# A written-out order of work, searched anew, and new places for the loads of xT and of the first state (one core, attention and rational FFN)

## The chip, the cores and the metric

The kernel runs on one core of a Trainium2 chip. The metric is the time on the device of one execution, in microseconds (us), smaller is better. The engines are TensorE (PE in the profile, its weight loads PEld), VectorE (DVE), ScalarE (ACT), GpSimd (POOL) and the queue SP, which issues most DMAs.

## The reference

For each of 8 batches and 8 heads, 512 tokens `x` (64 wide) attend to 32 state rows, and the state rows attend to the tokens. All rows, 4608 in sum and 512 wide, go through a feed-forward layer whose activation is a quotient of two polynomials.

```python
scores = scale * x @ state.T                     # 512 x 32 per head
a = softmax(scores); xread = a @ state           # 512 rows of a batch
a2 = softmax(scale * state @ x.T); sread = a2 @ x  # 32 rows of a batch
h = rows @ w_in                                  # rows: 4608 x 512, w_in: 512 x 2048
P = a0 + a1*h + a2*h*h + a3*h*h*h
Q = 1 + |b0|*|h| + |b1|*h*h
out = (P / (Q + 1e-6)) @ w_out                   # w_out: 2048 x 512
```

## The kernel before, in words

The work of the feed-forward layer is cut into 72 units. Units 0 to 63 are batch b = n//8 and slice u = n%8 of 256 of the 2048 hidden columns, over that batch's 512 tokens; units 64 to 71 are the eight slices for the 256 state rows of all batches. `xread` is never formed: for four batch pairs and eight slices the state is first multiplied with `w_in` (token `X:i`, function `extra`, tile `ps_x`; `XA` copies the result out of PSUM to `xo` or `xo_w`, `xs` stores it, `lm` loads it again), and a unit's h is the softmax times that product (token `F:n:ci`, function `front`, tile `h`). Every number that TensorE multiplies here is split in a high and a low part, so `F` has 12 matmuls of 512 columns for a unit of tokens.

What happens in a unit n after `F`:

- ACT reads h twice: `FB` makes A = |b1|-scaled |h|, `FC` makes C, both 128x1024.
- DVE makes the polynomials: `qd`, `mu`, `po`. ACT takes the absolute value (`qa`).
- ACT makes the reciprocal 1/Q as exp(-ln Q): `ln` (function `recip_ln`, activation Ln) and `ex` (function `recip_exp`, activation Exp).
- DVE multiplies, `g1` gives the high part gh; `g2` and `g3` prepare the low part; POOL makes gl (`gl`).
- PE adds to four output accumulators o0 to o3 of the batch: `mh:n:t` is 4 matmuls of 512 columns with gh, `ml:n:t` 2 with gl.

The weights come as 64-bit floats and are made into 32 bits on the core: `lr` loads (512 KB a half), `cp` is a Prelu on ACT, `jr` and `jl` are two DVE instructions, `wh` (ACT) and `wl` (POOL) split a slice of `w_out`, `ws` stores a slice of `w_in`. The attention of a batch has its own tokens (`scores`, `sc_copy`, `row_...`, `col_...`, `e2_T`, `e2_copy`, `sread`, `sr_copy`, `sr_T`, `sr_fin`); batch 0 has its own variants that end in 0. `sread` needs `e2T`, which `e2_copy` writes on ACT.

PSUM has two tiles with the tag `h`, which `F`, `X`, the scores and `sread` take in turn: who takes one waits until everything that reads what was in it before is done.

Nothing is scheduled by the machine. The list ORDER holds 2337 tokens, and `tc.manual_schedule()` emits them one after the other; each engine runs its own instructions in that order, waiting where an input or a buffer is not ready. ORDER is therefore the order on every engine and queue at once. One token, `pre`, emits an explicit load of the ACT function table that holds both Ln and Exp; before the change it is the second token of the list (after the load of the first two batches' state), and in the instructions as built it is the only `ACT_TABLE_LOAD`. Where no such load stands ahead of an activation, the building step puts one in.

The loads of `xT` and `x` are 512 KB each (half a batch), and before the change both turn through the two buffers of one tag "x", in an order worked out from the list (token `lx`).

Of the kernel before, what the change touches and what calls it, by code (L numbers as in the profile page):

```python
# [18 lines left out]
P = 128  # L19
# [4 lines left out]
    "ls:0:2 pre lx scores0:0 sc_copy0:0 lr:0:0 cp:0:0 row_T0:0 jr:0:0 jl:0:0 row_max0:0 row_sub0:0 lx "  # L24
    "scores0:1 sc_copy0:1 row_T0:1 row_exp0:0 lr:0:1 cp:0:1 jr:0:1 ls:2:8 col_max:0 jl:0:1 "
    "col_scale:0 col_exp:0:0 col_exp:0:1 row_max0:1 row_sub0:1 row_exp0:1 row_sum0:0 row_norm0:0 X:1 "
    "row_sum0:1 lr:1:0 cp:1:0 lr:1:1 jr:1 X:0 XA:1 XA:0 fh:0 fo:0 cp:1:1 jl:1 X:2 a_T0:0 XA:2 lc cb "
    "cv a_hi0:0 a_lo0:0 row_norm0:1 a_T0:1 a_hi0:1 a_lo0:1 e2_T0:1 lr:2:0 cp:2:0 lr:2:1 b0a jr:2 "
    "cp:2:1 jl:2 X:4 fh:1 XA:4 lr:4:0 cp:4:0 lr:3:0 cp:3:0 lr:3:1 lr:4:1 cp:3:1 F:0:0 F:0:1 FB:0 fo:1 "
    "col_eps:0 col_norm:0 F:1:0 F:1:1 lr:5:0 jr:3 jl:3 xs:1 jr:4 FC:0 wh:3 wl:3:0 wl:3:1 FB:1 qd:0 "  # L30
    "qa:0 e2_T0:0 ln:0 ex:0 e2_copy0:0 e2_copy0:1 mu:0 qd:1 cp:5:0 po:0 lr:5:1 jr:5 cp:5:1 xs:0 lx lx "
    "sread:0:0 g1:0 mh:0:2 ws:0 cp:4:1 qa:1 FC:1 lr:7:0 xs:4 g2:0 sread:0:1 sr_copy:0 mh:0:3 jl:5 "
    "wh:5 sr_T:0 sr_fin:0 g3:0 ln:1 ex:1 ws:1 mu:1 po:1 lr:7:1 X:5 XA:5 X:8 XA:8 gl:0 ml:0:2 jl:4 "
    "g1:1 fh:2 lr:6:0 fo:2 cp:7:0 jr:7 cp:6:0 mh:0:1 cp:7:1 lr:6:1 cp:6:1 X:9 F:2:0 g2:1 xs:2 xs:5 "
    "XA:9 F:2:1 FB:2 FC:2 wl:5:1 wl:5:0 mh:1:1 jl:7 wh:7 ws:2 xs:8 g3:1 X:6 XA:6 jr:6 gl:1 mh:0:0 "
    "ml:0:0 qd:2 qa:2 ln:2 ml:0:3 mu:2 po:2 mh:1:0 jl:6 lr:9:0 wl:7:1 ex:2 g1:2 X:12 fh:3 XA:12 "
    "lr:9:1 cp:9:0 cp:9:1 X:10 lr:8:0 lr:8:1 ml:0:1 fo:3 jr:9 xs:6 wl:7:0 lr:11:0 lr:11:1 cp:8:0 jr:8 "
    "cp:8:1 xs:9 g2:2 XA:10 ml:1:2 jl:9 xs:10 mh:1:3 g3:2 gl:2 ml:1:3 F:3:0 F:3:1 FC:3 FB:3 ws:3 X:16 "
    "fh:4 ml:1:0 mh:2:1 lr:10:0 jl:8 mh:2:0 XA:16 lr:10:1 mh:1:2 ml:1:1 wh:9 wl:9:1 wl:9:0 lr:12:0 "
    "qd:3 qa:3 ln:3 xs:12 fo:4 lx mh:2:3 mu:3 ex:3 po:3 cp:11:0 jr:11 X:13 XA:13 X:14 XA:14 ml:2:2 "  # L40
    "cp:11:1 cp:10:0 cp:10:1 g1:3 ml:2:0 jr:10 F:4:0 xs:14 F:4:1 FB:4 lr:12:1 g2:3 FC:4 jl:11 xs:16 "
    "X:20 XA:20 mh:3:1 g3:3 gl:3 jl:10 fh:5 lr:13:0 lr:13:1 ml:2:1 wh:11 qd:4 mh:3:3 ml:2:3 xs:20 "
    "qa:4 ln:4 mh:2:2 fo:5 F:5:0 wl:11:0 ex:4 cp:12:0 cp:12:1 F:5:1 FC:5 mu:4 po:4 jr:12 ws:4 X:17 "
    "ml:3:1 g1:4 g2:4 wl:11:1 lr:14:0 mh:4:1 mh:3:2 lr:14:1 XA:17 xs:17 X:21 lx cp:13:0 jr:13 cp:13:1 "
    "FB:5 g3:4 XA:21 ml:3:3 xs:13 mh:3:0 jl:12 qd:5 gl:4 mu:5 cp:14:0 mh:4:3 cp:14:1 jr:14 mh:4:2 "
    "ml:4:1 xs:21 ml:3:2 po:5 qa:5 ln:5 ex:5 jl:13 ws:6 g1:5 jl:14 X:25 XA:25 ml:3:0 xs:25 lr:15:0 "
    "g2:5 scores:1:0 scores:1:1 sc_copy:1 tr1:1 wh:13 wl:13:1 X:24 wl:13:0 fh:6 fo:6 X:29 XA:29 xs:29 "
    "row_max:1 ml:4:2 wh:14 wl:14:0 lr:15:1 col_max:1 row_sub:1 XA:24 g3:5 mh:4:0 col_scale:1 F:6:0 "
    "F:6:1 lm:8 FB:6 lx mh:5:2 row_exp:1 cp:15:0 lx X:28 XA:28 lw:0 mh:5:1 xs:28 ml:4:3 mh:5:0 ml:4:0 "
    "row_sum:1 mh:5:3 gl:5 ml:5:1 ml:5:0 qd:6 row_eps:1 row_norm:1:0 cp:15:1 jr:15 ws:7 lm:10 "  # L50
    "row_norm:1:1 fh:7 fo:7 fs:8 F:7:0 ml:5:2 FC:6 mu:6 ml:5:3 po:6 col_exp:1:0 col_exp:1:1 qa:6 ln:6 "
    "jl:15 wl:14:1 ex:6 ws:5 tr2:1 X:3 XA:3 F:7:1 e2_T:1 a_hi:1 g1:6 g2:6 FB:7 mh:6:3 mh:6:2 FC:7 "
    "ft:8 lm:9 mh:6:0 g3:6 gl:6 e2_copy:1 sread:1:0 sread:1:1 mh:6:1 wh:15 col_eps:1 wl:15:1 qd:7 "
    "wl:15:0 col_norm:1 fs:10 sr_copy:1 sr_T:1 mu:7 ml:6:3 qa:7 sr_fin:1 a_lo:1 ml:6:1 ln:7 ex:7 "
    "F:8:0 F:8:1 FB:8 FC:8 po:7 g1:7 g2:7 g3:7 lw:3 ml:6:0 ml:6:2 mh:7:0 qd:8 fs:9 qa:8 lx lx ft:9 "
    "mh:7:1 mh:7:3 ln:8 ex:8 mu:8 po:8 g1:8 g2:8 mh:7:2 g3:8 F:9:0 F:9:1 FC:9 gl:7 FB:9 qd:9 ml:7:1 "
    "fl:7:1 ml:7:2 ml:7:3 fl:7:2 ml:7:0 fl:7:0 ft:10 F:10:0 F:10:1 fl:7:3 mh:8:1 mh:8:2 FB:10 mu:9 "
    "lm:11 po:9 gl:8 mh:8:0 ml:8:0 mh:8:3 lm:12 fs:12 FC:10 mu:10 ft:12 F:12:0 F:12:1 fs:11 ft:11 "
    "qa:9 ln:9 ex:9 FB:12 qd:10 qa:10 ml:8:3 po:10 F:11:0 F:11:1 FC:12 g1:9 mh:9:0 mh:9:2 xs:24 g2:9 "
    "g3:9 lw:6 mh:9:3 ml:8:1 qd:12 mh:9:1 gl:9 ml:9:2 lw:1 ml:9:1 ln:10 mu:12 ex:10 g1:10 g2:10 "  # L60
    "ml:8:2 FB:11 mh:10:3 mh:10:0 po:12 ml:9:3 FC:11 lm:13 fs:13 lm:15 ft:13 X:7 g3:10 gl:10 fs:15 "
    "qa:12 ft:15 mh:10:1 ml:9:0 ln:12 ex:12 xs:3 qd:11 mu:11 mh:10:2 XA:7 xs:7 ml:10:3 qa:11 ln:11 "
    "ml:10:2 lw:4 g1:12 mh:12:2 scores:2:0 ex:11 scores:2:1 po:11 g1:11 g2:11 g3:11 gl:11 sc_copy:2 "
    "col_max:2 X:15 XA:15 mh:12:0 lm:16 lw:2 F:13:0 F:13:1 FC:13 ml:10:0 tr1:2 row_max:2 row_sub:2 "
    "lm:14 lx lx fs:14 ft:14 mh:12:3 FB:13 qd:13 mh:11:3 X:11 XA:11 ml:11:1 xs:11 g2:12 row_exp:2 "
    "qa:13 ln:13 mh:11:2 col_scale:2 ex:13 ml:10:1 os:7:1 mh:12:1 ml:11:0 ml:11:3 F:14:0 col_exp:2:0 "
    "F:14:1 g3:12 col_exp:2:1 FB:14 gl:12 ml:12:0 ml:12:1 fs:16 ml:12:3 mu:13 po:13 g1:13 mh:13:0 "
    "F:15:0 F:15:1 g2:13 row_sum:2 row_eps:2 FC:14 mh:11:1 ml:11:2 os:7:0 qd:14 qa:14 row_norm:2:1 "
    "mh:13:3 ml:12:2 mh:13:2 ft:16 ln:14 ex:14 os:7:2 mh:11:0 row_norm:2:0 FB:15 mu:14 po:14 os:7:3 "
    "g3:13 mh:13:1 tr2:2 a_hi:2 e2_T:2 qd:15 qa:15 xs:15 lm:18 gl:13 ml:13:3 ml:13:0 e2_copy:2 FC:15 "  # L70
    "g1:14 mh:14:0 ln:15 a_lo:2 F:16:0 F:16:1 FC:16 mh:14:2 mh:14:3 g2:14 g3:14 mh:14:1 FB:16 gl:14 "
# [993 lines left out]
```

## Time and profile before

| | us |
|---|---|
| time, median of 3 runs (lowest, highest) | 664.37 (663.86, 664.41) |
| time of the execution that was profiled | 663.79 |
| its span, from the first to the last instruction | 662.0 |
| PE busy in the span | 644.4 |
| DVE busy | 624.6 |
| ACT busy | 521.4 |
| POOL busy | 314.3 |

The profiled execution's own time is 1.79 us longer than its span. An engine's busy time says how much of the span it was at work; what an engine waits for, and when, is read from the timelines and the windows. Line numbers are those of the kernel before; from the changed functions on the same lines of the changed kernel are numbered one or two away.

### The profile page before, as it was taken

How to read it: one execution, taken by the hardware profiler on the slowest of the kernel's cores; microseconds unless marked ns; L12 is line 12 of the kernel's file. 1: busy time of each engine (PE TensorE's matmuls, PEld its weight loads, DVE VectorE, ACT ScalarE, POOL GpSimd, SP SyncE). 2: the span in 40 equal slices, each digit the busy share in tenths (PEclk: the TensorE clock that was granted, in tenths of full speed). 3: DMA queues.
4: the chain of work that ended last, by engine and by line, in shares of the span. 5: the costliest groups of instructions: out<-in, count | busy, mean ns of one | idle time of the engine just before them, and what ended most of it. 6: DMA issues, size and time to landing. Idle time of an engine off the chain costs nothing.

```text
span 662.0 us, 11300 instructions
## 1 busy us (share of the span) xinstructions
PE 644.4 (97%) x4474; PEld 509.8 (77%) x4474; DVE 624.6 (94%) x585; ACT 521.4 (79%) x633; POOL 314.3 (47%) x174
## 2 busy tenths in 40 slices
PE   6699999999999999999999999999999999999997
PEld 2566767877877777877878888878878888888895
DVE  5999999999998999999999999999999999999886
ACT  5998989897869778878787778877787778687573
POOL 1164447545445165545444465436453555445541
PEclk9899999999999999999999999999999999999999
DMA  8979887316303365221123320431402201121401
GB/s 353 401 265 337 301 299 250 133 65 249 133 20 111 109 215 184 65 80 52 60 80 118 122 93 36 143 112 32 128 33 100 77 17 48 33 64 49 141 36 32
DMA packets 30679, 85.67 MB, mean 129 GB/s; under 512 B 3490, under 2 KB 3618, under 8 KB 30626
## 3 DMA queue, kind: packets, MB, share of 16 engines
q1 hardware_dynamic: 30290, 84.56, 36.6%
q8 instruction: 35, 0.57, 0.4%
q10 hardware_dynamic: 336, 0.39, 0.2%
q14 instruction: 18, 0.15, 0.1%
HBM read 57.15 MB, written 27.79 MB: 128 GB/s over the span
## 4 chain that ended last, share of the span: by engine, by line
PE 91%; ACT 3%; DVE 3%; issue 2%; DMA 1%; DVEq 0%
PE h L817 29%; PE ps_x L714 4%; PE o__2202 L890 2%; PE o__1510 L890 2%; PE o__1492 L890 2%; PE o__4162 L890 2%; PE o__4153 L890 2%; PE o__2245 L890 2%; PE o__2194 L890 2%; PE o__1517 L890 2%; PE o__3564 L890 2%; PE o__4771 L890 2%; PE o__2263 L890 2%; PE o__3531 L890 2%; PE o__5313 L890 2%; PE o__5820 L890 2%
## 5 line engine op out<-in xcount | busy, mean ns | idle before, releaser
L880 POOL TENSOR_TENSOR gl<-C,L 128x1024 fp32r<-128x1024 f32 (+1 forms) x70 | 176.0, 2514 | 252.7 <-DVE C L873 161.4
L817 PE MATMUL h<-aT,m 128*128 128x512 f32 x768 | 186.4, 391 | 0.8 <-DVE m L750 0.6
L817 PEld LDWEIGHTS h<-aT,m 128*128 128x128 f32 x768 | 143.3, 188 | 33.9 <-DVE m L750 1.7
L836 ACT ACTIVATE A<-h,cst 128x1024 f32<-128x1024 f32 (+1 forms) x72 | 76.9, 1070 | 43.4 <-PE h L817 37.4
L861 DVE SCALAR_TENSOR_TENSOR gh<-C,cst,L 128x1024 fp32r<-128x1024 f32 (+1 forms) x72 | 97.3, 1351 | 10.1 <-ACT L L937 8.1
L829 ACT ACTIVATE C<-h,cst 128x1024 f32<-128x1024 f32 (+1 forms) x72 | 83.4, 1159 | 25.8 <-PE h L817 19.0
L763 POOL TENSOR_TENSOR m<-m_sb,m 128x512 fp32r<-128x512 f32 x56 | 82.7, 1486 | 37.3 <-ACT m L759 33.7
L873 DVE SCALAR_TENSOR_TENSOR C<-C,cst,A 128x1024 f32<-128x1024 f32 (+1 forms) x72 | 89.2, 1242 | 1.5
L850 DVE SCALAR_TENSOR_TENSOR A<-A,b0a,h 128x1024 f32<-128x1024 f32 (+1 forms) x72 | 87.0, 1214 | 3.6 <-ACT A L836 2.6
L844 DVE SCALAR_TENSOR_TENSOR C<-C,cst,h 128x1024 f32<-128x1024 f32 (+1 forms) x72 | 87.7, 1218 | 1.7
L867 DVE SCALAR_TENSOR_TENSOR A<-A,gh 128x1024 f32<-128x1024 f32 (+1 forms) x72 | 85.8, 1193 | 1.5
L840 DVE TENSOR_TENSOR C<-C,h 128x1024 f32<-128x1024 f32 (+1 forms) x72 | 83.0, 1153 | 3.3 <-ACT C L829 2.0
L856 ACT ACTIVATE A<-A 128x1024 f32<-128x1024 f32 (+1 forms) x72 | 73.0, 1014 | 15.2 <-DVE A L850 14.5
L927 ACT ACTIVATE L<-A 128x1024 f32<-128x1024 f32 (+1 forms) x72 | 73.0, 1014 | 5.9 <-POOL gl L880 2.1
L937 ACT ACTIVATE L<-L 128x1024 f32<-128x1024 f32 (+1 forms) x72 | 72.9, 1014 | 1.8
L714 PE MATMUL ps_x<-win_sb,st 64*32 64x256 f32 x1024 | 36.3, 396 | 1.1 <-DVE C L844 0.4
L759 ACT CAST m<-m_sb 128x512 fp32r<-128x512 f32 x56 | 33.8, 615 | 0.0
L352 POOL TENSOR_TENSOR wo<-cv_r,wo 128x512 fp32r<-128x512 f32 x16 | 23.5, 1489 | 15.0 <-ACT wo L345 8.9
L714 PEld LDWEIGHTS ps_x<-win_sb,st 64*32 64x32 f32 x1024 | 17.6, 109 | 16.4 <-issue 5.8
L732 ACT COPY xo<-ps_x 128x1024 f32<-128x1024 f32 (+1 forms) x24 | 20.9, 875 | 5.1 <-PE ps_x L714 4.9
L817 PEld LDWEIGHTS h<-sh,m 128*128 128x128 f32 x192 | 24.1, 191 | 0.6
L817 PE MATMUL h<-sh,m 128*128 128x256 f32 x192 | 24.3, 283 | 0.0
(244 smaller groups left out, 1104.0 us busy)
## 6 DMA issues: line engine op xcount, KB each, us to landing
m_sb<-m_dram SPq DMA_DIRECT2D x56, 256.0 KB, 3.3
xT_sb<-in_xT_dram SPq DMA_DIRECT2D x16, 512.0 KB, 4.7
x_sb<-in_x_dram SPq DMA_DIRECT2D x16, 512.0 KB, 5.7
m_dram<-xo SPq DMA_DIRECT2D x16, 512.0 KB, 3.8
win_sb<-w_in_dram SPq DMA_DIRECT2D x16, 512.0 KB, 4.7
out_dram<-o_sb SPq DMA_DIRECT2D x32, 256.0 KB, 3.5
raw<-in_w_in_dram SPq DMA_DIRECT2D x10, 512.0 KB, 7.2
raw_w<-in_w_out_dram SPq DMA_DIRECT2D x8, 512.0 KB, 8.2
```

Of the source, the lines that this page charges most:

```text
L714: nc.tensor.matmul(ps[k * NS : (k + 1) * NS, j, q, :], st[j * D : (j + 1) * D, 2 * e + q, k, :], win_t[u][j * D : (j + 1) * D, k, :], star ...
L763: nc.gpsimd.tensor_tensor(m[:, 1], MF.pop(n), m[:, 0].bitcast(F32), op=ALU.subtract)
L817: nc.tensor.matmul(h[:, ci * W : (ci + 1) * W], l, r, start=(q == 0), stop=(q == len(seq) - 1),)
L829: nc.scalar.activation(e["C"], e["h"], AF.Identity, scale=cst[:, 3:4], bias=cst[:, 2:3])
L840: nc.vector.tensor_tensor(e["C"], e["C"], e["h"], op=ALU.mult)
L844: nc.vector.scalar_tensor_tensor(e["C"], e["C"], cst[:, 1:2], e["h"], op0=ALU.add, op1=ALU.mult)
L850: nc.vector.scalar_tensor_tensor(e["A"], e["A"], b0a, e["h"], op0=ALU.add, op1=ALU.mult)
L861: nc.vector.scalar_tensor_tensor(e["gh"], e["C"], cst[:, 0:1], e["L"], op0=ALU.add, op1=ALU.mult)
L867: nc.vector.scalar_tensor_tensor(e["A"], e["A"], 1.0 + 1e-6, e["gh"].bitcast(F32), op0=ALU.add, op1=ALU.mult)
L873: nc.vector.scalar_tensor_tensor(e["C"], e["C"], cst[:, 0:1], e["A"], op0=ALU.add, op1=ALU.subtract)
L880: eng.tensor_tensor(e["gl"], e["C"], e["L"], op=ALU.mult)
L890: nc.tensor.matmul(O[t], e[l][:, j * W + x : j * W + x + P], WO[u][:, j, k, :], start=(u == 0 and l == "gh" and k == 0 and j == 0), stop=( ...
```

## The change

The list ORDER is replaced. Both lists have 2337 tokens; apart from the loads of x, xT and the state they hold the same tokens, in another order. Beside that:

- `lx`, which loaded the next of x and xT, is replaced by `lx:b:g` (x) and `lt:b:g` (xT), so that the list itself says what is loaded where. xT of batches 4 to 7 goes into the two buffers of the tag "xo", which the copied state products used before; xT of batches 0 to 3 and all of x stay in the two buffers "x".
- The state was loaded as batches 0 and 1 (on the ACT queue) and 2 to 7 (on SP); it is now loaded as batch 0 alone and 1 to 7.
- In the new list `pre` stands after `mh:0:0`, behind the first two units' `ln` and `ex`.

```diff
 ORDER = [
-    "ls:0:2 pre lx scores0:0 sc_copy0:0 lr:0:0 cp:0:0 row_T0:0 jr:0:0 jl:0:0 row_max0:0 row_sub0:0 lx "
+    "lt:0:0 lc ls:0:1 scores0:0 sc_copy0:0 lr:0:0 row_T0:0 cp:0:0 jr:0:0 jl:0:0 cb row_max0:0 "
...
+    "fh:2 X:5 XA:5 fo:2 cp:7:0 lr:7:1 jr:7 cp:7:1 xs:2 mh:0:0 pre xs:4 g2:1 wl:5:0 XA:8 cp:6:1 ml:0:0 "
...
-    xseq, x_at = [], [0]
-
-    def load_next_x():
-        i = x_at[0]
-        if i == len(xseq):
-            return
-        x_at[0] += 1
-        what, b, g = xseq[i]
-        if what == "xT":
-            t = ld.tile([P, NP, S // 2], F32, name="xT_sb", tag="x")
-            nc.sync.dma_start(t, xT[b, g])
-        else:
-            t = ld.tile([P, NT // 2, DM], F32, name="x_sb", tag="x")
-            nc.sync.dma_start(t, x[b, g])
-        X[xseq[i]] = t
+    def load_xT(b, g):
+        pool, tag = (ld, "x") if b < 4 else (ew, "xo")
+        t = X["xT", b, g] = pool.tile(
+            [P, NP, S // 2], F32, name="xT_sb", tag=tag, bufs=2
+        )
+        nc.sync.dma_start(t, xT[b, g])
+
+    def load_x(b, g):
+        t = X["x", b, g] = ld.tile(
+            [P, NT // 2, DM], F32, name="x_sb", tag="x", bufs=2
+        )
+        nc.sync.dma_start(t, x[b, g])
...
-        "lx": load_next_x,
+        "lx": load_x,
+        "lt": load_xT,
```

On ACT, from the first unit's |A| (`qa:0`) to the second half of the `w_in` conversion that follows, these rows stood in the program before (Ln is the row `L<-A`, Exp is `L<-L`, the rows `cv_y<-raw` are conversions, `e2T` is what `sread` needs):

```order
L856 ACTIVATE A<-A 128x1024
L927 ACTIVATE L<-A 128x1024
L937 ACTIVATE L<-L 128x1024
L624 COPY e2T<-ps_e_349 128x512
L624 COPY e2T<-ps_e_252 128x512
L299 ACTIVATE cv_y<-raw 128x512 x3
```

In the changed program the same place reads:

```order
L855 ACTIVATE A<-A 128x1024
L926 ACT_TABLE_LOAD
L926 ACTIVATE L<-A 128x1024
L936 ACT_TABLE_LOAD
L936 ACTIVATE L<-L 128x1024
L301 ACTIVATE cv_y<-raw 128x512
L623 COPY e2T<-ps_e_242 128x512
L623 COPY e2T<-ps_e_263 128x512
L301 ACTIVATE cv_y<-raw 128x512
```

A table load now stands ahead of Ln and another ahead of Exp, and one conversion moved ahead of the copies to `e2T`.

Further on ACT, from the copies `sr` of batch 0's state read to the copy of the state product of `X:5` (first row `xo_w`), before the change:

```order
L649 ACTIVATE sr<-ps_sr,r_145 128x64 x2
L345 CAST wo<-cv_r 128x2x512
L660 COPY srT<-ps_sr 128x4x32
L927 ACTIVATE L<-A 128x1024
L937 ACTIVATE L<-L 128x1024
L732 COPY xo_w<-ps_x 128x1024
L732 COPY xo<-ps_x 128x512
L746 CAST m<-ps_x 128x512
```

And in the changed program, up to the load that the token `pre` emits (L947):

```order
L648 ACTIVATE sr<-ps_sr,r_137 128x64 x2
L926 ACT_TABLE_LOAD
L926 ACTIVATE L<-A 128x1024
L301 ACTIVATE cv_y<-raw 128x512
L301 ACTIVATE cv_y<-raw_w 128x512
L659 COPY srT<-ps_sr 128x4x32
L936 ACT_TABLE_LOAD
L936 ACTIVATE L<-L 128x1024
L347 CAST wo<-cv_r 128x2x512
L745 CAST m<-ps_x 128x512
L731 COPY xo_w<-ps_x 128x1024
L301 ACTIVATE cv_y<-raw_w 128x512 x2
```

Unit 1's Ln with its table load and two conversions moved ahead of the copy `srT`, and a second load stands ahead of Exp; `L947 ACT_TABLE_LOAD` is the row behind the last one shown. One more load, at the very start, takes the place of the one of `pre` there; the program has six in all.

On PE, from `sread` of batch 0 (tile `ps_sr`) to the third unit's `F` (the row `h<-aT,m ... x12`), before the change:

```order
L637 MATMUL ps_sr<-x_sb,e2T 32x64 x16
L890 MATMUL o__393<-wo,gh 128x512 x4
L637 MATMUL ps_sr<-x_sb,e2T 32x64 x16
L890 MATMUL o__426<-wo,gh 128x512 x4
L655 MATMUL ps_sr<-ident,sr 128x128
L714 MATMUL ps_x<-win_sb,st 32x256 x32
L890 MATMUL o__393<-wo,gl 128x512 x2
L890 MATMUL o__502<-wo,gh 128x512 x4
L714 MATMUL ps_x<-win_sb,st 32x256 x16
L817 MATMUL h<-aT,m 128x512 x12
```

And in the changed program:

```order
L636 MATMUL ps_sr<-x_sb,e2T 32x64 x32
L889 MATMUL o__409<-wo,gh 128x512 x4
L654 MATMUL ps_sr<-ident,sr 128x128
L713 MATMUL ps_x<-win_sb,st 32x256 x32
L889 MATMUL o__492<-wo,gh 128x512 x4
L889 MATMUL o__492<-wo,gl 128x512 x2
L816 MATMUL h<-aT,m 128x512 x12
```

One group of 4 with gh and one state product of 16 rows (32 matmuls in the trace) moved from ahead of the third unit's `F` to behind it. The first 16 rows of `ps_x` are now `X:8`, which takes the PSUM tile that `srT` is copied from, and `F` takes the tile that `xo_w` (of `X:5`) is copied from.

## Rows read from the trace of the kernel before

**Rows 1.** The page's busy times: us, share of the span, instructions.

```profile
PE 644.4 (97%) x4474; PEld 509.8 (77%) x4474; DVE 624.6 (94%) x585; ACT 521.4 (79%) x633; POOL 314.3 (47%) x174
```

**Rows 2.** Windows: us, busy us (instructions) by engine, clock, DMA share, GB/s.

```profile
20.00:30.00 10.00, 5.72 (x27) 4.36 (x25) 9.76 (x13) 9.94 (x14) 2.50 (x2) 0.94 1.00 399
...
40.00:60.00 20.00, 19.28 (x218) 12.71 (x217) 19.38 (x19) 17.47 (x24) 7.95 (x5) 1.00 0.92 328
60.00:100.00 40.00, 39.47 (x443) 27.01 (x442) 39.89 (x39) 36.63 (x47) 20.14 (x11) 1.00 0.88 311
...
400.00:500.00 100.00, 100.00 (x558) 81.08 (x556) 97.54 (x87) 79.50 (x92) 51.27 (x26) 1.00 0.25 82
```

**Rows 3.** Timeline of PE, 25 to 45 us: start, us, instruction, [idle before, releaser].

```profile
25.12 0.60 PE L536 MATMUL ps_e<-ident,e 128*128 128x128 f32 x4
30.45 1.35 PE L637 MATMUL ps_sr<-x_sb,e2T 128*32 128x64 f32 x32 [4.73 <-ACT e2T L624]
31.74 2.07 PE L890 MATMUL o__393<-wo,gh 128*128 128x512 f32 x4
...
36.22 0.27 PE L655 MATMUL ps_sr<-ident,sr 128*128 128x128 f32 x1
36.84 1.96 PE L714 MATMUL ps_x<-win_sb,st 64*32 64x256 f32 x64 [0.35 <-ACT srT L660]
...
40.31 1.09 PE L714 MATMUL ps_x<-win_sb,st 64*32 64x256 f32 x32
41.64 3.02 PE L817 MATMUL h<-aT,m 128*128 128x512 f32 x12 [0.23 <-DVE m L750]
```

**Rows 4.** Timeline of ACT, the start and 24 to 40 us.

```profile
1.19 1.28 ACT L948 ACT_TABLE_LOAD   x1 [1.19 <-PEq L1047]
...
26.58 1.17 ACT L856 ACTIVATE A<-A 128x1024 f32<-128x1024 f32 x1
27.78 1.06 ACT L927 ACTIVATE L<-A 128x1024 f32<-128x1024 f32 x1
28.87 1.06 ACT L937 ACTIVATE L<-L 128x1024 f32<-128x1024 f32 x1
29.83 1.05 ACT L624 COPY e2T<-ps_e 128x512 f32<-128x512 f32 x2
30.77 1.83 ACT L299 ACTIVATE cv_y<-raw 128x512 f32<-128x512 f32 x3
32.47 1.08 ACT L856 ACTIVATE A<-A 128x1024 f32<-128x1024 f32 x1
33.42 1.23 ACT L829 ACTIVATE C<-h,cst 128x1024 f32<-128x1024 f32 x1
34.89 0.52 ACT L649 ACTIVATE sr<-ps_sr,r 128x64 f32<-128x64 f32 x2 [0.24 <-PE ps_sr L637]
35.30 1.05 ACT L345 CAST wo<-cv_r 128x1024 fp32r<-128x1024 f32 x1
36.52 0.27 ACT L660 COPY srT<-ps_sr 128x128 f32<-128x128 f32 x1 [0.18 <-PE ps_sr L655]
...
38.74 0.99 ACT L732 COPY xo_w<-ps_x 128x1024 f32<-128x1024 f32 x1
```

**Rows 5.** Windows of 2 us around the gap on PE, columns as in rows 2.

```profile
28.00:30.00 2.00, 0.00 (x0) 0.00 (x0) 2.00 (x3) 1.97 (x3) 0.37 (x1) 0.72 1.02 410
...
34.00:36.00 2.00, 2.00 (x36) 1.62 (x29) 2.00 (x2) 1.76 (x4) 0.73 (x1) 0.57 0.89 350
```

**Rows 6.** Timeline of DVE: gh of the first two units.

```profile
30.25 1.28 DVE L861 SCALAR_TENSOR_TENSOR gh<-C,cst,L 128x1024 fp32r<-128x1024 f32 x1
...
38.87 2.11 DVE L861 SCALAR_TENSOR_TENSOR gh<-C,cst,L 128x1024 fp32r<-128x1024 f32 x1
```

**Rows 7.** Groups of PE by form: all the scores; busy us, mean ns, idle before, releaser.

```profile
L396 PE MATMUL ps_sc<-xT_sb,st 64*32 64x256 f32 x256 | 9.9, 413 | 4.9 <-DMA st<-in_stT_dram 4.9
```

**Rows 8.** Timeline of PE at 17 us: the spread of the constants.

```profile
17.08 0.38 PE L249 MATMUL ps_c<-row,ones 1*128 1x6 f32 x2 [0.19 <-DVE m L750]
```

More of the change, by code (lines that the diff above doesn't have):

```diff
@@ L1007, in attention_rational_ffn @@
             early_x.add(args[0])
-    for name, args in tokens:
-        if name in ("scores0", "scores", "sread"):
-            b, g = (0, *args)[-2:]
-            xseq.append(("x" if name == "sread" else "xT", b, g))
     with tc.manual_schedule():
```

339 rows, old and new, of the table ORDER are left out of this document.

## The prediction

> **What bounds the kernel now.** I read the page's busy times first: PE is at work for 644.4 of 662.0 us, DVE for 624.6, ACT for 521.4 [rows 1]. The windows say where the rest is. From 100 us on PE is full (the hundred from 400 to 500 us shows 100.00), while DVE has some slack and ACT a fifth [rows 2]. Between 40 and 100 us PE is busy for 58.75 of 60 us and DVE for 59.27 of 60, so DVE has nothing to spare there [rows 2]. Between 20 and 30 us it is another picture: PE 5.72 of 10 us, ACT 9.94 [rows 2]. So what PE does not do before 40 us it can't catch up later, and before 40 us ACT decides. The timeline of PE shows the place: after its 25.12 row it stands still for 4.73 us until ACT has copied e2T, then waits 0.35 us for the copy srT and 0.23 us for a split on DVE; in sum 5.3 us [rows 3]. ACT runs through that stretch with gaps of 0.24 and 0.18 us only [rows 4].
>
> **What the change can't move.** Both lists hold the same work, so PE's, DVE's and POOL's busy times stay. xT's new tiles: the scores waited for 4.9 us in the whole run, all of it for the first state, never for xT [rows 7]; a transfer that nobody waits for gains nothing when it may start earlier, and I put it at 0. The smaller first state: 64 KB less ahead of the first scores is 0.16 us at the 399 GB/s of the windows [rows 2]. Against it the constants' spread moves between the first transposes and the second scores, 0.38 us [rows 8]. From there to 25 us both lists put the same instructions before ACT in nearly the same order; I take 0 for this part, with 0.3 us to either side.
>
> **The table loads.** What is left is the order on ACT. `pre` made the one table load, at 1.19 us, 1.28 us long, while ACT waited for the first scores anyway [rows 4]. Now Ln and Exp of the first two units each have a load ahead of them, and `pre` makes a fifth extra one. None has cover: ACT is full there. Behind the first stand, on ACT, Ln, Exp, a conversion and the copies to e2T, for which PE waits, and gh on DVE.
>
> I step through ACT with the distances between starts in [rows 4]. |A| of unit 0 ends at 27.75 as before. A load (1.28) and Ln (28.87 - 27.78 = 1.09) end at 30.12, a load and Exp (29.83 - 28.87 = 0.96) at 32.36. A conversion (a third of 32.47 - 30.77, 0.57) comes first now: 32.93. sread began 0.62 us after the first e2T copy started (29.83 to 30.45), so now at 33.55 instead of 30.45: 3.1 us later. PE's gap is 7.8 us long instead of 4.73.
>
> Then on ACT: the e2T copies to 33.87 (0.94), a conversion 34.44, C of unit 1 (1.23) 35.67, |A| (0.95) 36.62, sr (0.41) 37.03, a load 38.31, Ln 39.40, two conversions 40.54, and only then srT. PE meanwhile has sread's two halves (about 1.3 us each), 4 matmuls with gh (2.0) and the transpose (0.27): done at 38.45 [rows 3]. Its next instruction, the state product of X:8, wants the tile that srT is copied from, and starts 0.32 us after srT as before (36.52 to 36.84): 40.86. That is a new gap of 2.4 us where 0.35 stood. PE then has 64 rows of state products (1.96), 4 matmuls with gh and 2 with gl (6 at 3.02/12, less the pipeline's end: 1.4) and is dry at 44.2. The third unit's F wants the copy xo_w: a load after srT 42.05, Exp 43.0, the cast wo (1.0) 44.0, a cast of half its size (0.5) 44.5, the copy (1.0) 45.5. A third gap, 1.3 us instead of 0.23.
>
> The sum of gaps is 11.5 us instead of 5.3: 6.2 more. The other way to count: F starts at 45.5 instead of 41.64, 3.9 later, and PE owes what was moved behind it, 4 matmuls (0.95) and a state product (1.09): 5.9. I take **6.0**. The fifth load comes after that copy, and what waits behind it (the copy of X:8) is needed by PE only after F and ten matmuls with gh and gl, some 5 us on; cover holds, 0, and 1.3 us if it were gone.
>
> **The price of one load, from both sides.** The only row is 1.28 us on an idle engine [rows 4]. Less than nothing is excluded: a load makes no data earlier. Below: 0, if the engine fetched the table while the activation ahead runs. Above: a load must also break the overlap of neighbours, some 0.1 us on each side (28.87 lies 0.03 after the end of the row ahead, 29.83 lies 0.1 before it), so 1.5; or, as the farthest row, it drains the activation ahead, one full 1.06 us more, 2.34. I take 1.28, since it is a row of the same instruction. The Trainium skill's page "ScalarE: Activation LUTs", section "What ACT_TABLE_LOAD costs", gives 1283 ns for the load, as this trace shows, and 1380 ns of drain with it, which no row here shows; by it the four loads would cost about 5.5 us more and the time would be near 676.
>
> **What comes after.** gh of unit 0 can start at 32.5 instead of 30.25, and gh of unit 1 at 43.1 instead of 38.87 [rows 6]: DVE is 4.2 us late where it has nothing to spare, PE 6.0. So PE stays the one behind, and PE's idle 1.0 us between 42 and 100 us is the most that can be given back; I credit 0.5. The clock: in the first gap the granted clock fell from 2.4 to 1.2 GHz at 28.9 us (0.72 in its window) and came back at 35.7 (0.57) [rows 5], 5.2 us after PE had started again. Now PE starts again at 33.55 and stands again at 38.45, after 4.9 us, so the clock may still be at 1.2 GHz from 40.86 on: the 3.4 us of work until 44.2 would take 6.8, of which 1.3 lies under the third gap, 2.1 more. It may also be back; I take 1.0 between 0 and 3 (the third unit's F too).
>
> Sum: 6.0 - 0.5 + 1.0 = 6.5. The profiled execution took 663.79, 1.79 more than its span, and the median is 664.37; that gives 670.3 to 670.9, and I say **670.6**. The likeliest case's own range goes from DVE's 4.2 (668) to 6.2 + 3 (673).
>
> **The rivals.**
> - A load costs 2.3 us where it stands between dependent activations, the upper price above. For it: a row of 1.28 on an idle engine says nothing of an engine in full run. Against: Ln and Exp follow their inputs within 0.03 us [rows 4], so ACT's pipe is short. Four loads on the path by 1.06 more: 4.2 us, 675.
> - The loads aren't there, or cost nothing. Then e2T's copies are 0.57 late, F starts at about 40.4 and owes 2.0: 0.8 us, 665.2: no change that could be told, so not slower. It decides as soon as the trace shows one table load, or Ln and Exp a microsecond apart. Against: the program as built has six where it had one, and of the one before the trace shows exactly one [rows 4]. The Trainium skill's page "ScalarE activation tables: per-element evaluation and per-set limits", section "Table sets in the compiler and the runtime", says that the back end places loads by the greedy longest run; by that the first set would hold both Ln and Exp and this case would come true. The changed program's listing does not agree.
> - The later list lets PE wait where it didn't. For it: over 2000 tokens stand elsewhere, with PE at 100.00. Against: DVE has 2.5 us of slack in that hundred [rows 2]. A wait of 1 us in each of seven batches gives 677 to 678.
> - Faster: only if no load counts and the gap at 25 us closes as well; e2T's copies stand behind Exp in both lists, so I see nothing that would close it.
>
> **Chances.** Forecast 0.68, dear loads 0.11, no loads 0.10, later waits 0.07, faster 0.04. What this kernel's measurement can tell from no change is about 0.2%, 1.3 us (663.0 to 665.7). Of the case without loads I count 0.08 as the same and 0.01 on either side. Faster 0.05, same 0.08, slower 0.87. The range, 666.0 to 677.5, leaves out the cases without slowing and half of the last waits.
>
> **What would show it.** Right: five more ACT_TABLE_LOAD rows of 1.28 us between 27 and 50 us; gaps of about 7.8, 2.4 and 1.3 us on PE before the third unit's F, which starts near 45.5; a second stretch at half clock; PE at 100 from 100 us on. Wrong: loads longer than 1.5 us, or Ln right behind |A|; a PE that is short of full in the later windows; DVE, not PE, full to the end.

## The result, and the profile after

| | before | after |
|---|---|---|
| time, median of 6 executions each (lowest, highest), us | 664.07 (663.14, 664.41) | 668.67 (668.20, 669.46) |
| time of the profiled execution | 663.79 | 669.24 |
| its span | 662.0 | 667.5 |
| mean granted clock of PE in it, share of full speed | 0.994 | 0.987 |

The changed kernel is slower by 4.6 us: ratio 1.0073, 95% interval 1.0063 to 1.0083. The two profiled spans lie 5.5 us apart: the profiled execution lies 0.3 us below the median before and 0.6 above it after. Three of the six executions after had a clock of 0.987, as the profiled one, and took 669.04 to 669.46; the three at 0.990 to 0.992 took 668.20 to 668.31.

The page's busy times after:

```profile
PE 644.8 (97%) x4474; PEld 511.8 (77%) x4474; DVE 622.0 (93%) x585; ACT 527.5 (79%) x638; POOL 311.2 (47%) x174
```

ACT has five instructions more than in [rows 1] and 6.1 us more work; PE and DVE have as many instructions and nearly the same time. The windows after, columns as in [rows 2]:

```profile
20.00:30.00 10.00, 6.24 (x40) 4.31 (x24) 9.76 (x12) 9.97 (x14) 2.50 (x2) 0.97 0.89 320
30.00:40.00 10.00, 4.38 (x69) 3.07 (x69) 7.70 (x8) 9.94 (x13) 1.66 (x1) 0.50 0.95 383
40.00:60.00 20.00, 18.47 (x214) 12.27 (x222) 17.27 (x15) 19.20 (x25) 9.74 (x6) 0.84 0.51 173
60.00:100.00 40.00, 39.58 (x471) 27.16 (x456) 39.55 (x39) 38.24 (x48) 17.48 (x10) 1.00 0.97 347
400.00:500.00 100.00, 100.00 (x558) 81.15 (x556) 95.09 (x84) 77.21 (x89) 49.10 (x25) 1.00 0.23 72
```

Between 30 and 40 us ACT is full while PE works for 4.38 us and DVE for 7.70; PE's clock is at the lower level, 0.50, all through it. From 60 us on the picture is that of before. The timeline of ACT after shows with what it is full (columns as in [rows 4]):

```profile
27.42 1.13 ACT L855 ACTIVATE A<-A 128x1024 f32<-128x1024 f32 x1
28.57 1.28 ACT L926 ACT_TABLE_LOAD   x1
29.86 1.06 ACT L926 ACTIVATE L<-A 128x1024 f32<-128x1024 f32 x1
30.93 1.28 ACT L936 ACT_TABLE_LOAD   x1
32.23 1.06 ACT L936 ACTIVATE L<-L 128x1024 f32<-128x1024 f32 x1
33.19 0.65 ACT L301 ACTIVATE cv_y<-raw 128x512 f32<-128x512 f32 x1
33.74 1.05 ACT L623 COPY e2T<-ps_e 128x512 f32<-128x512 f32 x2
...
37.85 1.28 ACT L926 ACT_TABLE_LOAD   x1
39.14 1.06 ACT L926 ACTIVATE L<-A 128x1024 f32<-128x1024 f32 x1
...
41.22 0.26 ACT L659 COPY srT<-ps_sr 128x128 f32<-128x128 f32 x1
41.49 1.28 ACT L936 ACT_TABLE_LOAD   x1
42.79 1.06 ACT L936 ACTIVATE L<-L 128x1024 f32<-128x1024 f32 x1
...
45.30 1.01 ACT L731 COPY xo_w<-ps_x 128x1024 f32<-128x1024 f32 x1
46.21 1.27 ACT L301 ACTIVATE cv_y<-raw_w 128x512 f32<-128x512 f32 x2
47.50 1.28 ACT L947 ACT_TABLE_LOAD   x1
```

A sixth load of 1.28 us stands at 1.19 us, as before. Each of the other five starts within 0.03 us of the end of the instruction ahead, and Ln and Exp follow each within 0.02 us. The copies to e2T start at 33.74 instead of 29.83, srT at 41.22 instead of 36.52 [rows 4]. The timeline of PE after shows who waits for them (columns as in [rows 3]):

```profile
20.22 6.02 PE L816 MATMUL h<-aT,m 128*128 128x512 f32 x24
34.36 2.21 PE L636 MATMUL ps_sr<-x_sb,e2T 128*32 128x64 f32 x64 [8.12 <-ACT e2T L623]
36.50 2.08 PE L889 MATMUL o__409<-wo,gh 128*128 128x512 f32 x4
...
41.53 3.67 PE L713 MATMUL ps_x<-win_sb,st 64*32 64x256 f32 x64 [2.74 <-ACT srT L659]
45.12 1.84 PE L889 MATMUL o__492<-wo,gh 128*128 128x512 f32 x4
...
47.27 2.89 PE L816 MATMUL h<-aT,m 128*128 128x512 f32 x12
```

Where gaps of 4.73, 0.35 and 0.23 us stood [rows 3], there are 8.12 and 2.74, and no third. The 64 state products take 3.67 us where they took 1.96: the clock is at half. The third unit's F (last row) starts at 47.27 instead of 41.64. DVE's wait in the same place (timeline of DVE, gh of the first two units, as in [rows 6]):

```profile
33.32 1.28 DVE L860 SCALAR_TENSOR_TENSOR gh<-C,cst,L 128x1024 fp32r<-128x1024 f32 x1 [2.23 <-ACT L L936]
...
43.88 1.28 DVE L860 SCALAR_TENSOR_TENSOR gh<-C,cst,L 128x1024 fp32r<-128x1024 f32 x1 [1.85 <-ACT L L936]
```

Both wait for Exp, and the second comes 5.0 us later than before. One difference in time lies before this stretch: F of unit 0 starts at 20.22 where it started at 19.44, 0.8 us late.

### The profile page after: what moved, and what is told of

It reads as the page before. It is cut to its first block, busy times and chain, and to the rows that moved or that the text cites. A ratio compares the mean times of both kernels' runs of the same rounds, so it can differ in the third digit from the quotient of the medians.

```text
span 667.5 us, 11314 instructions
## 1 busy us (share of the span) xinstructions
PE 644.8 (97%) x4474; PEld 511.8 (77%) x4474; DVE 622.0 (93%) x585; ACT 527.5 (79%) x638; POOL 311.2 (47%) x174
## 4 chain that ended last, share of the span: by engine, by line
PE 87%; DVE 5%; ACT 5%; issue 2%; POOL 1%; DMA 1%; POOLq 0%; ACTq 0%
PE h L816 27%; PE ps_x L713 5%; PE o__492 L889 2%; PE o__1523 L889 2%; PE o__1537 L889 2%; PE o__2243 L889 2%; PE o__1504 L889 2%; PE o__2212 L889 2%; PE o__2971 L889 2%; PE o__4158 L889 2%; PE o__4756 L889 2%; PE o__2234 L889 2%; PE o__4149 L889 2%; PE o__4133 L889 2%; PE o__2268 L889 2%; PE o__4121 L889 2%
## 5 line engine op out<-in xcount | busy, mean ns | idle before, releaser
L879 POOL TENSOR_TENSOR gl<-C,L 128x1024 fp32r<-128x1024 f32 (+1 forms) x70 | 174.2, 2491 | 239.8 <-DVE C L872 143.0
L860 DVE SCALAR_TENSOR_TENSOR gh<-C,cst,L 128x1024 fp32r<-128x1024 f32 (+1 forms) x72 | 93.2, 1294 | 15.1 <-ACT L L936 10.9
L762 POOL TENSOR_TENSOR m<-m_sb,m 128x512 fp32r<-128x512 f32 x56 | 79.9, 1435 | 40.1 <-ACT m L758 33.8
L866 DVE SCALAR_TENSOR_TENSOR A<-A,gh 128x1024 f32<-128x1024 f32 (+1 forms) x72 | 88.7, 1234 | 1.6
L872 DVE SCALAR_TENSOR_TENSOR C<-C,cst,A 128x1024 f32<-128x1024 f32 (+1 forms) x72 | 87.6, 1223 | 1.7
L504 POOL TENSOR_TENSOR e<-e,rs 128x512 f32<-128x512 f32 x14 | 17.6, 1275 | 19.4 <-DVE r L470 7.9
```

The costliest lines, as they stand in the source:

```text
L762: nc.gpsimd.tensor_tensor(m[:, 1], MF.pop(n), m[:, 0].bitcast(F32), op=ALU.subtract)
L860: nc.vector.scalar_tensor_tensor(e["gh"], e["C"], cst[:, 0:1], e["L"], op0=ALU.add, op1=ALU.mult)
L866: nc.vector.scalar_tensor_tensor(e["A"], e["A"], 1.0 + 1e-6, e["gh"].bitcast(F32), op0=ALU.add, op1=ALU.mult)
L872: nc.vector.scalar_tensor_tensor(e["C"], e["C"], cst[:, 0:1], e["A"], op0=ALU.add, op1=ALU.subtract)
L879: eng.tensor_tensor(e["gl"], e["C"], e["L"], op=ALU.mult)
```

## The experiments

All are compared with the kernel before, run on the same chip in the same session; its medians there were 663.43 (e1 to e4), 663.73 (e5 to e8) and 663.64 (e9 to e12). Diffs of the list show only the tokens around an edit.

### e1: the changed kernel with `pre` first

```diff
-lt:0:0 lc ls:0:1 scores0:0 ... xs:2 mh:0:0 pre xs:4
+lt:0:0 lc ls:0:1 pre scores0:0 ... xs:2 mh:0:0 xs:4
```

> The changed kernel with one token moved: pre (the load of the table with Ln and Exp) stands behind the first state load instead of behind mh:0:0, so one ACT_TABLE_LOAD is left of six. Theory, the five extra loads on ACT are what costs: the front gets back what the loads took there (the gaps of 8.12 and 2.74 us on PE shrink to about 5 and under 1), the time falls by 4 to 6 us to 663 to 665. Rival, the new order of the other tokens costs and the loads lie beside it: the time stays within 1.5 us of 668.7.

Measured: 663.37 us, ratio 1.0007 [0.9998, 1.0016] to the kernel before; span 661.3. PE's timeline in e1:

```profile
31.66 2.20 PE L639 MATMUL ps_sr<-x_sb,e2T 128*32 128x64 f32 x64 [5.58 <-ACT e2T L626]
...
37.40 1.96 PE L716 MATMUL ps_x<-win_sb,st 64*32 64x256 f32 x64 [1.72 <-ACT srT L662]
...
40.79 2.94 PE L819 MATMUL h<-aT,m 128*128 128x512 f32 x12
```

One token's place is the whole loss: with it first, the new list, the new xT tiles and the small first state together take as long as the kernel before. Between e1 and after the two ratios differ by 0.66%, 4.4 us. The new list's own order still makes a longer first gap than before (5.58 for 4.73) and a second of 1.72.

### e2: the kernel before with `pre` late

```diff
-ls:0:2 pre lx scores0:0 ... gl:1 mh:0:0 ml:0:0
+ls:0:2 lx scores0:0 ... gl:1 mh:0:0 pre ml:0:0
```

> The kernel before with one token moved: pre stands behind mh:0:0, as in the new list, so the same five loads come in on the old order. Theory, the loads are the cost: PE's gap before sread grows from 4.73 to about 7.3 us, F of the third unit starts some 4 to 5 us later, and the time rises by 4 to 6 us to 668 to 670. Rival, the order of the other tokens is the cost: within 1.5 us of 664.1.

Measured: 670.56 us, ratio 1.0109 [1.0095, 1.0123]; span 668.8. PE's timeline in e2:

```profile
32.91 1.35 PE L641 MATMUL ps_sr<-x_sb,e2T 128*32 128x64 f32 x32 [7.27 <-ACT e2T L628]
...
45.30 1.57 PE L718 MATMUL ps_x<-win_sb,st 64*32 64x256 f32 x32 [2.09 <-ACT xo_w L736]
```

The old list pays for the same loads too, 7.1 us, so it isn't the new list that makes them dear. Its first gap grew by 2.54, two loads; the second pair shows at another place, the copy xo_w.

### e3: two loads of the same table in the kernel before

```diff
-qa:0 e2_T0:0 ln:0 ex:0 e2_copy0:0
+qa:0 e2_T0:0 pre ln:0 pre ex:0 e2_copy0:0
```

> The kernel before with two more loads of the very same table, one ahead of Ln and one ahead of Exp of unit 0 only. Theory, a load costs its own 1.28 us on ACT and no drain: PE's first gap grows by 2.56 us to 7.3, the time rises by 2 to 3.5 us to 666 to 667.5. Rival, a load costs 2.3 to 2.7 us where activations depend on each other: the gap grows by 4.6 to 5.4 and the time rises by over 4.5 us. Second rival, loading the table that is already there costs nothing: 664.1.

Measured: 665.98 us, ratio 1.0037 [1.0024, 1.0049], 2.55 us; span 664.2. ACT's timeline in e3:

```profile
26.53 1.08 ACT L860 ACTIVATE A<-A 128x1024 f32<-128x1024 f32 x1
27.63 1.28 ACT L952 ACT_TABLE_LOAD   x1
28.93 1.06 ACT L931 ACTIVATE L<-A 128x1024 f32<-128x1024 f32 x1
30.00 1.28 ACT L952 ACT_TABLE_LOAD   x1
31.30 1.06 ACT L941 ACTIVATE L<-L 128x1024 f32<-128x1024 f32 x1
```

This prices one load in the full stream: 1.28 us in the row and 1.28 in the time. The dear load of 2.3 us is out. These two load the table that is already there, and that costs as much as the load at the start (1.28 us, [rows 4]). The Trainium skill's page "ScalarE: Activation LUTs", section "What ACT_TABLE_LOAD costs", adds a drain of 1380 ns for a switch to a different set; if that held here, two loads would be an estimated 5.3 us. No drain shows in these rows, nor at the four loads that the building step put ahead of Ln and Exp in the changed kernel (0.01 to 0.03 us on either side), and the measurement decides.

### e4: state and xT tiles alone

```diff
-ls:0:2 pre lx ... ls:2:8 col_max:0
+ls:0:1 pre lx ... ls:1:8 col_max:0
-            t = ld.tile([P, NP, S // 2], F32, name="xT_sb", tag="x")
+            pool, tag = (ld, "x") if b < 6 else (ew, "xo")
+            t = pool.tile([P, NP, S // 2], F32, name="xT_sb", tag=tag, bufs=2)
```

> The kernel before, its list kept but for the state being loaded as batch 0 alone and then 1 to 7, and with xT of batches 6 and 7 in the tiles of the copied state products (for batches 4 and 5 the old order does not allow it). Theory: neither is waited for, so within 0.5 us of 664.1. Rival, the first state alone starts the scores earlier and the whole moves with it: 0.2 to 0.5 us faster; or the shared tiles make a load of xT wait: slower by 0.5 us or more.

Measured: 663.31 us, ratio 0.9998 [0.9989, 1.0007]; span 662.3. In the old order only batches 6 and 7 were moved; with the first state alone this is worth nothing either way. For batches 4 and 5 e1 stands, where all of it together is worth nothing.

### e5: the constants' spread back behind the scores (on e1)

```diff
-lt:0:0 lc ls:0:1 pre ... jl:0:0 cb ... cv b0a row_max0:1 ... lr:1:1 cp:1:0 ... XA:2 e2_T0:0
+lt:0:0 ls:0:1 pre ... jl:0:0 ... row_max0:1 ... lr:1:1 lc cp:1:0 ... XA:2 cb cv b0a e2_T0:0
```

> The changed list with pre first and, beside that, the spread of the constants (two matmuls on PE, their copy and b0a on ACT, their load on SP) put back to behind the third state product, as in the old list. Theory: in the new place the spread stands between the first transposes and the second scores and sets the whole front back, so that F of the first unit, which came 0.78 us late, comes back to 19.4 to 19.6 us and the time falls by 0.4 to 0.8 us against the run with pre first (663.4). Rival, the time of the front is set by ACT behind that: under 0.2 us.

Measured: 664.54 us, ratio 1.0012 [1.0003, 1.0020]; span 661.9. A miss: the second scores came back to 7.66 us (8.39 in after), but the spread then had to wait for its PSUM tile at 17.4 us, and F of unit 0 started at 20.67 instead of 20.09. The new wait of 1.07 us and the spread's 0.38 stand ahead of that F, so this run can't tell whether the 0.8 us of the start part is the spread's doing.

### e6: five loads in the middle of the kernel before

```diff
+pre ahead of ln:20, ln:24, ln:28, ln:36 and ln:44
```

> The kernel before with five more loads of the same table, each ahead of Ln of a unit in the middle (20, 24, 28, 36, 44), where PE is full and ACT has a fifth of its time free. Theory, a load costs only where ACT is the one that is waited for: within 0.5 us of 663.5 although ACT is busy 6.4 us longer. Rival, each load delays the chain of its unit and PE waits for it: 1.28 us each, 669 to 670.

Measured: 669.75 us, ratio 1.0090 [1.0074, 1.0105]; span 666.9. A miss: ACT's free time there doesn't hide the loads, but the five didn't cost alike. Against before, F of unit 24, behind the first load (235.2 us), is late by 0.4; that of unit 32, behind three, by 4.6; that of unit 48, behind all five, by 4.9. The largest group of PE's waits between 200 and 480 us in e6 (us in total, times, longest):

```profile
PE h L821 <- DVE C L848: 2.3, 2, 2.0
```

One wait of 2.0 us makes most of it, F's for the DVE instruction that reads its PSUM tile; in before the only such wait there is 0.3 us.

### e11: only the third of those five

```diff
-qa:28 ln:28
+qa:28 pre ln:28
```

> The kernel before with one more load of the same table, ahead of Ln of unit 28 (near 305 us). In the run with five such loads the time rose by 6.0 us, and F came to be late by 4.2 us between units 24 and 32. Theory, this one load makes nearly all of it, because PE already waited for DVE at that place before the change: the time rises by 3.5 to 5 us. Rival, each of the five costs its 1.2 us: 1 to 1.5 us.

Measured: 668.12 us, ratio 1.0064 [1.0050, 1.0078]; span 664.9. One load of 1.28 us costs 2.9 us in the profiled execution and 4.5 by the medians. Timelines of ACT, DVE and PE in e11:

```profile
303.27 1.28 ACT L952 ACT_TABLE_LOAD   x1
...
306.76 1.28 DVE L865 SCALAR_TENSOR_TENSOR gh<-C,cst,L 128x1024 fp32r<-128x1024 f32 x1 [0.90 <-ACT L L941]
...
316.52 1.06 ACT L860 ACTIVATE A<-A 128x1024 f32<-128x1024 f32 x1 [2.72 <-DVE A L854]
...
317.82 2.97 PE L821 MATMUL h<-aT,m 128*128 128x512 f32 x12 [1.97 <-DVE C L848]
```

The load makes Exp late; on DVE gh, which stands in the list's order ahead of the next unit's polynomials, waits for Exp, and what is behind it waits too; 14 us later F wants the PSUM tile whose reader stands behind those, and PE stops for 1.97 us. In before the same F started at 315.42 without a wait. But the wait for Exp is the smaller part: gh starts 0.49 us later than in before, the reader of the tile 2.85 later (316.41 for 313.56). The rest are two DVE instructions that are longer than in before. First DVE and POOL in before, then in e11:

```profile
308.85 1.28 DVE L873 SCALAR_TENSOR_TENSOR C<-C,cst,A 128x1024 f32<-128x1024 f32 x1
308.99 2.31 POOL L763 TENSOR_TENSOR m<-m_sb,m 128x512 fp32r<-128x512 f32 x1 [3.81 <-ACT m L759]
```

```profile
309.21 1.29 POOL L767 TENSOR_TENSOR m<-m_sb,m 128x512 fp32r<-128x512 f32 x1 [4.43 <-ACT m L763]
309.34 2.23 DVE L877 SCALAR_TENSOR_TENSOR C<-C,cst,A 128x1024 f32<-128x1024 f32 x1
...
312.63 1.54 DVE L421 TENSOR_SCALAR cm<-cm 128x2 f32<-128x2 f32 x1
```

In before DVE's instruction starts 0.14 us ahead of POOL's, and POOL's is the long one; in e11 it starts 0.13 behind, and DVE's is longer by 0.95. The second, `cm`, took 0.16 us in before; here it ends with the POOL instruction that runs beside it (gl, 311.75 to 314.15), 1.38 longer. e6 has the same two rows (2.25 and 1.55 us). By these rows the load shifts DVE by half a microsecond, and that lets POOL come first; no run tests this by itself. So the price of 1.28 us of ACT is set by what the shift meets: 0.4 ahead of unit 20's Ln, 1.28 in e3, 2.9 and more here.

### e7: PE kept at work in its two gaps (changed kernel)

```diff
+        "wm": warm,     # k matmuls of 512 columns that nobody reads
-F:1:1 wl:3:0 ... sr_T:0 ln:1
+F:1:1 wm:7 wl:3:0 ... sr_T:0 wm:3 ln:1
```

> The changed kernel, all six loads in place, with 7 matmuls of 512 columns whose product nobody reads in PE's first gap and 3 in its second, so that PE is at work there. It adds work that the reference doesn't have and leaves nothing out. Theory, the half clock adds to the loss of the gaps: the granted clock stays at 2.4 GHz or comes back earlier, the state products take 1.96 instead of 3.67 us, F of the third unit then waits for the copy xo_w (end 46.3) and starts at about 46.4 instead of 47.27, so the time falls by 0.5 to 1 us. Second theory, the clock's loss counts in full: 1.8 us or more. Rival, the clock is not among the causes: within 0.3 us of 668.7.

Measured: 668.69 us, ratio 1.0072 [1.0060, 1.0085]; span 667.0. A window of e7, columns as in [rows 2]:

```profile
30.00:40.00 10.00, 6.76 (x79) 3.35 (x78) 7.71 (x8) 9.93 (x14) 1.40 (x1) 1.00 0.96 388
```

The third unit's F in e7 (timeline of PE):

```profile
46.50 3.04 PE L820 MATMUL h<-aT,m 128*128 128x512 f32 x12 [1.16 <-ACT xo_w L735]
```

With matmuls in the gaps the granted clock stays at 2.4 GHz, and the third unit's F starts 0.8 us sooner, at 46.5, although F of unit 0 starts 0.26 later than in after. It now waits for the copy xo_w. The expected gain in time didn't come: the median is that of after. So the half clock is worth about a microsecond at F, and in the time nothing that can be told.

### e8: the new list mended by hand (on e1 and e5)

```diff
+e2_copy0:0 e2_copy0:1 now ahead of ln:0; sr_copy:0 sr_T:0 behind cp:5:1; sr_fin:0 behind qa:1;
+mh:0:0 mh:0:1 behind X:8, mh:0:3 cp:6:0 behind XA:5
```

> A version meant to beat both: the new list with pre first, the spread late, the copies of e2T ahead of Ln, the copies sr and srT earlier on ACT, one conversion behind the third unit's first copy, and three groups of gh matmuls of unit 0 pulled ahead to where PE stood still. Theory: sread starts near 30.4 instead of 31.66, the gap of 1.72 us before the state products closes, F of the third unit starts near 40.5 with 1.4 us less work owed, and the time falls to 661 to 662.3. Rival, DVE, full until 100 us, sets the pace and PE waits later instead: 663 to 664.

Measured: 664.89 us, ratio 1.0018 [1.0009, 1.0027]; span 662.9. A miss. PE has 8 matmuls of 512 columns done ahead of the third unit's F that e1 has behind it, and F starts 0.9 us later than in e1, so PE is ahead; but gh of unit 1 is 1.0 us later than in e1 (40.3 for 39.3), since Ln and Exp of unit 0 now stand behind the copies and DVE runs behind from there on, and the span is 1.6 longer.

### e9 and e10: work added to DVE, and to PE (each on e1)

```diff
+e9:  a DVE max over 128x1024, nobody reads it, behind g2:1, g2:2 and g2:3
-e10:         for q in range(2):
+e10:         for q in (0, 1) * (2 if i in (13, 14, 17) else 1):   # these X twice
```

> The changed list with pre first and three instructions more on DVE between 45 and 75 us (a maximum over the state, 128x1024, some 1.21 us each, read by nobody), 3.6 us in all. It leaves nothing out. Theory, DVE sets the pace from 30 to 115 us: the time rises by 3 to 4 us, to 666.4 to 667.5. Rival, PE sets it and DVE has time to spare: under 1 us.

> The changed list with pre first and three of the state products (X:13, X:14, X:17, between 50 and 75 us) made twice, 3.2 us more on PE, into the same tile with the same result. Theory, DVE sets the pace there and PE has between 1 and 2 us of waits and thin stretches up to 115 us: the time rises by 1 to 2.2 us. Rival, PE sets the pace: 3.2 us.

Measured: e9 673.11 us, ratio 1.0142 [1.0129, 1.0155], span 671.5; e10 666.42 us, ratio 1.0039 [1.0026, 1.0052], span 663.5. The added DVE work (e9, answer for its line: min/median/max ns, first and last start in us):

```profile
L953 DVE TENSOR_REDUCE scrap<-st x3: 1203/1205/1208, 44.6 to 70.9; 128x2 f32<-128x1024 f32 x3
```

In e9 the first F of unit 4 is 2.4 us later than in e1, behind two of the three (2.4 us), and that of unit 8 is 3.6 later, behind all three (3.6 us): DVE had nothing to spare there. In e10, 3.2 us more of PE work became 2.2 us of span: PE had 1 us to spare. The rest of e9's loss, 6.6 us, comes after unit 8 and is no wait. A window with the same work in e1 and then in e9, columns as in [rows 2]:

```profile
114.00:213.00 99.00, 99.00 (x663) 78.96 (x662) 93.98 (x83) 82.87 (x96) 49.63 (x28) 1.00 0.41 140
```

```profile
117.60:218.00 100.40, 100.40 (x663) 79.10 (x662) 93.90 (x82) 83.09 (x96) 49.57 (x28) 1.00 0.41 138
```

PE is full in both, at the full clock, and needs 1.4 us longer for the same 663 matmuls. The reason is open. e9 therefore tells something of DVE up to unit 8 only.

### e12: integer work moved to POOL (on e1)

```diff
-        nc.vector.tensor_scalar(
+        (nc.gpsimd if 6 <= g <= 13 else nc.vector).tensor_scalar(
```

> A version meant to beat both: the changed list with pre first, and eight of the sixteen conversions jr (groups 6 to 13, 0.69 us each on DVE, between 40 and 100 us) given to POOL, which is at work for half of that time; 5.5 us less on DVE. Theory, DVE sets the pace until 115 us and PE can go 1 to 2 us faster before it is full: 661 to 662.5. Rival, POOL's own work (gl, the low parts) comes later for it and PE waits for that: 663.4 or more.

Measured: 682.49 us, ratio 1.0285 [1.0272, 1.0299]. A miss. One of the two forms of the moved instruction on POOL in e12:

```profile
L317 POOL TENSOR_SCALAR cv_r<-raw_w x4: 3692/4682/4777, 39.5 to 79.2; 128x1024 int32<-128x1024 uint32 x4
```

On DVE it takes 0.69 us, on POOL 3.7 to 4.8, and PE then waits for the low part of w_out, up to 4.2 us at once. No version ran faster than the kernel before; e1 equals it.

## Why the prediction was right, and where it was off

The time was forecast as 670.6 and is 668.67, within the forecast case's own range (668 to 673) and near its lower end. Point by point:

**Where and by what: right.** Five more loads, on a full ACT; PE stands and can't catch up. e1 shows that the loads' place in the list makes the loss, e2 that they make one in either list, e3 that one costs its 1.28 us there. The rival without loads falls by the rows and the rival of dear loads by e3. The rival of later waits falls by the distances below.

**The gaps: nearly right.** Forecast 7.8, 2.4 and 1.3, seen 8.12, 2.74 and none. The third was to be the wait for xo_w; half clock made the work ahead of F last until then, so it is covered; at full clock, in e7, it is there with 1.16. In sum 5.55 us more than before, where 6.0 was taken.

**xT's tiles and the first state: 0, right; the start part: 0.8 late, taken as 0.** e4 shows the first, for batches 6 and 7. F of unit 0 is late in e1 too, so it belongs to the list; which of its tokens is to blame stays open after e5.

**The fifth load: 0, right.** It stands at 47.50, behind the copy xo_w; PE's next wait for a copied state product is 0.3 us in after and in e1 alike.

**The clock: 1.0, about right.** PE's third F is 5.63 us later: 0.78 from the start, 5.55 from the gaps, less the 2.04 of work that moved behind it; 1.34 is left for the half clock. e7 gives back 0.8 of it at F, and by the medians nothing that can be told.

**What PE gives back: the step that failed.** The prediction took PE's idle 1.0 us between 42 and 100 us as the most that can be given back, and credited 0.5. By the terms above PE was 7.67 us behind at the third F (5.63 late and 2.04 owed); the span is 5.5 longer; 2.2 came back. The starts in the profiled executions (timelines of PE and DVE, us) show where:

| kernel | third unit's F | gh of unit 1 | fifth unit's F | span | fifth F to the end |
|---|---|---|---|---|---|
| before | 41.6 | 38.9 | 66.7 | 662.0 | 595.3 |
| e3 | 43.8 | 40.8 | 68.9 | 664.2 | 595.3 |
| e1 | 40.8 | 39.3 | 66.0 | 661.3 | 595.3 |
| e8 | 41.7 | 40.3 | 67.7 | 662.9 | 595.2 |
| e7 | 46.5 | 44.1 | 71.8 | 667.0 | 595.3 |
| after | 47.3 | 43.9 | 72.1 | 667.5 | 595.3 |

The last column says that in these executions all is decided by the fifth unit's F: behind it all take the same time, although the kernels with the new list (the last four rows) still owe 6 matmuls of 512 columns there. Within one list the end follows the third F: e3 is 2.2 later there and 2.2 at the end, e7 against e1 5.7 and 5.7, after against e1 6.5 and 6.2. So the loads' loss is given back by 0.3 us only, as credited. The 2 us belong to the list: e1 is 0.85 earlier at the third F and owes 2.04, 1.2 behind by that count, and ends 0.7 ahead. Windows from the third unit's F to that of unit 8, where no work is owed any more (both lists then have the same matmuls behind them), and from there to the end, first before, then after (columns as in [rows 2]):

```profile
41.64:114.22 72.58, 71.56 (x775) 49.87 (x776) 71.78 (x72) 66.56 (x87) 36.19 (x21) 1.00 0.86 305
114.22:662.00 547.78, 543.21 (x3315) 442.15 (x3313) 519.22 (x472) 421.38 (x495) 266.09 (x141) 1.00 0.27 90
```

```profile
47.27:120.19 72.92, 72.50 (x812) 51.44 (x811) 71.76 (x71) 68.03 (x87) 37.11 (x21) 1.00 0.82 286
120.19:667.50 547.31, 542.75 (x3315) 442.64 (x3313) 515.85 (x471) 420.43 (x496) 263.59 (x141) 1.00 0.28 92
```

Three parts make the 2.2. PE's idle time in the first stretch falls from 1.02 to 0.42 us: 0.6, within the bound. The owed work, priced at 2.04, adds only 0.94 to PE's busy time there: 1.1. Behind unit 8 the same matmuls take 0.5 less. The second part belongs to the list: PE is busy for 71.6 us in that stretch in e3, e4, e6 and e11 too, and for 72.4 to 72.8 in e1, e5 and e7. The third may not: with the old list the way from unit 8 to the end took between 547.4 (e2) and 548.0 (e4). So the bound failed because it counted idle time alone, while the work moved behind a point was counted at its full duration. Why PE takes less time for that work in the new list isn't shown; e9's pair, where it takes more for the same matmuls, says that a PE at 100.00 and full clock has no fixed time for them.

**PE or DVE.** The expectations of e9, e10 and e12 held that DVE alone, full between 30 and 115 us, sets the end. The table speaks against it: in after DVE's gh is 4.6 later than in e1, PE's F 6.5, and the end 6.2. But e8, with PE ahead and DVE 1.0 behind, ended 1.6 late, and e9 lost all of DVE's added time at once. What fits all of them is the prediction's reading that both are full there and that the one further behind counts, with PE having about 1 us to spare (e10). By the ratios after costs 4.4 us more than e1, which lies at DVE's 4.6, not PE's 6.5; executions of one kernel lie over 1 us apart, so this is not settled.

**From the profiled execution to the median.** The profiled execution was 0.6 us above its median after, and 0.3 below it before. Of the 1.9 us that the forecast was off, this makes 0.9; the rest is the credit (1.7 too small) and the gaps (0.5 too large), less the start part (0.8) and the clock (0.3). That the sum lies within 2 us is partly luck: errors of 1.1 us one way (start part and clock) hid half of those of 2.2 the other way (credit and gaps).

## What to carry to other kernels

Look in the instructions as built for table loads whenever an order changes: an explicit load of a table that holds all functions must stand ahead of the first of them, and here the place of that one token was worth 4.4 us. Before pricing what a stall costs, look for the engine that is full behind it: on a full engine a short wait can go through to the end one for one (e3), and where the shift puts a DVE instruction behind one of POOL it can cost more than its own length (e11). When work is only put off past a stall, don't add its duration to the loss without seeing what stands at its new place.

## What the runs showed of the hardware that was not expected

- Loading the table that is already in place takes 1.28 us as any other load does (e3, e11), with at most 0.03 us of idle time on either side of it.
- PE at 100.00 and full clock needed 100.4 us in e9 for matmuls that took 99.0 in e1. The cause is open.
- A 128x1024 uint32 to int32 TENSOR_SCALAR takes 0.69 us on DVE and 3.7 to 4.8 us on POOL (e12).
- A DVE SCALAR_TENSOR_TENSOR that takes 1.28 us and a POOL TENSOR_TENSOR that takes 1.29 started within 0.14 us of each other in before, e6 and e11: each time the one that started second took 2.2 to 2.3 us.
